# Reordered copies, GpSimd work and last tiles in a fused attention and mixer kernel (Trainium2, one core)

## The chip, the cores and the metric

The kernel runs on one core of one Trainium2 chip. The metric is the device time of one execution in microseconds (us), as the median of the executions that agree. TensorE is called PE (its weight loads PEld), VectorE DVE, ScalarE ACT, GpSimd POOL; SP issues the DMAs. A ratio is the mean time of one kernel's fast runs over that of before's fast runs of the same rounds, so it is not quite the ratio of the medians that are quoted.

## The reference, cut to what matters

```python
# q, k, v: (4, 8, 768, 64) float32; lam: (8,)
# 1. lightning attention, blocks of 64 rows, state kv carried along the sequence
out[blk] = ((q @ k.T) * Dmask) @ v + (q * lam_pow) @ kv_state
kv_state = lam_block * kv_state + (k * rev_pow).T @ v
x = out.transpose(0, 2, 1, 3).reshape(4, 768, 512)
# 2. low-rank mixing along the sequence (rank 32), then a two-layer channel product
u = x + ((x.T @ U) @ V).T                       # U, V, w_ch1, w_ch2 come as float64
y = u + maximum(u @ w_ch1, 0) @ w_ch2           # (4, 768, 512) float32
```

## The kernel before

There are 24 steps of attention, one per tile of 128 rows (4 batches of 6). A step prepares the next tile (`prep`: q and k transposed by PE, copied out of PSUM by ACT), makes the outputs of its own tile, the scores of the next, and turns its result back (`back`). A batch that is complete is mixed (`mix`: x becomes u) and turned (`turn`: u transposed for the first product and split into a high part H, a low part, and a correction D), one tile per step. The last x tiles are mixed and turned between matmuls of the first product (`rest`: unit, matmul, piece; a unit has 24 matmuls).

The names in the traces: PE transposes q and k into pq and pk, ACT copies these to qt and kt, and GpSimd scales them to qs and ks. pss are the scores, which DVE masks to sm; px is the output of attention, xt its copy on ACT, pxn the tile turned back, x_nat its copy on ACT (`back`). pkv is the new state, kvc and kv its copies. pp and pr make the low-rank sum (pt, pt_h and vp are its copies), pu is what `mix` adds to x_nat on DVE ("the add"). put holds the transposes of `turn`; ut is its high part, made on DVE, u_hl holds H and the low part, te is ut scaled, uf a plain copy of put, and u_d is D (in a DMA line it is u stored to HBM). pz and pd are the two sums of the first product, and r is made of both, first on ACT, then on DVE.

```python
def prep(s):
    ...                       # PE: transposes pq, pk;  ACT: copies qt, kt
    ks = ...; nc.gpsimd.tensor_tensor(out=ks, in0=raw[s, "k"], ...)
    qs = ...; nc.gpsimd.tensor_tensor(out=qs, in0=qt, in1=powq, op=ALU.mult)
    for name in "qk":
        load_next(name)       # loads three tiles ahead; a buffer is free when ks has read it

def turn(s):
    ...                       # PE: transposes put
    nc.vector.tensor_scalar(t, pt, HI, ...)                      # DVE: ut
    nc.scalar.copy(uhl[g][:, 0, :, cols], t)                     # ACT: H
    low, diff = uhl[g][:, 1, :, cols], ud[g][:, :, cols]
    if g >= FG:                                                  # the last eight tiles
        nc.scalar.copy(uf, pt)                                   # ACT, reads PSUM
        nc.gpsimd.tensor_tensor(out=low, in0=uf, in1=t, ...)
        nc.vector.scalar_tensor_tensor(diff, t, 1.0 + E, pt, ...)  # D, reads PSUM
    else:
        nc.vector.tensor_tensor(out=low, in0=pt, in1=t, ...)
        nc.scalar.mul(te, t, E)
        nc.gpsimd.tensor_tensor(out=diff, in0=te, in1=low, ...)  # D
    nc.sync.dma_start(out=u_d[s], in_=xs.pop(s))                 # store of u

# step s: prep(s+1), mix, [low], outputs(s), [low_sum], scores(s+1), back(s), turn
# side work (decoding float64 weights) before scores or at the end of a step
rest = [
    (0, 0, "mix", c0 - 1), (0, 1, "turn", c0 - 2), (0, 5, "low", b), (0, 10, "low_sum", b),
    (0, 18, "mix", c0), (1, 0, "turn", c0 - 1), (1, 2, "mix", c0 + 1), (1, 8, "turn", c0),
    ...                       # turnings 8 matmuls apart, each tile mixed two turnings ahead
]
```

V was loaded in two halves, each broadcast to 128 partitions and decoded by itself. x tiles live in a ring of eight buffers.

## Time and profile before

| stretch | us | what bounds it |
|---|---|---|
| start to pss of step 1 | 11.76 | loads, decay masks |
| attention (to pss of step 23) | 132.47 | PE, with some 10 us of waits |
| head of the first product (to its fourth unit) | 35.69 | DVE's chain on the last tiles |
| rest of the products | 526.88 | PE without a wait |
| span | 706.80 | device time 708.66 |

In a timeline line stand start, duration, engine, source line, operation, output<-input, shapes and count, and in brackets how long the engine sat idle before it and what it waited for. "Idle time" of PE has to be read with care, because the profile models a matmul's end; I go by starts.

### The profile page before, as it was taken

How to read it: one execution, taken by the hardware profiler on the slowest of the kernel's cores; microseconds unless marked ns; L12 is line 12 of the kernel's file. 1: busy time of each engine (PE TensorE's matmuls, PEld its weight loads, DVE VectorE, ACT ScalarE, POOL GpSimd, SP SyncE). 2: the span in 40 equal slices, each digit the busy share in tenths (PEclk: the TensorE clock that was granted, in tenths of full speed). 3: DMA queues.
4: the chain of work that ended last, by engine and by line, in shares of the span. 5: the costliest groups of instructions: out<-in, count | busy, mean ns of one | idle time of the engine just before them, and what ended most of it. 6: DMA issues, size and time to landing. Idle time of an engine off the chain costs nothing.

```text
span 706.8 us, 11409 instructions
## 1 busy us (share of the span) xinstructions
PE 687.7 (97%) x4176; PEld 556.3 (79%) x4176; DVE 506.5 (72%) x909; ACT 305.8 (43%) x545; POOL 111.7 (16%) x91
## 2 busy tenths in 40 slices
PE   7999999998999999999999999999999999999997
PEld 6878797866788888888888888888888888888886
DVE  5668786866699877777779625678676586775864
ACT  4667677753466544444446412232232232322320
POOL 4324464632200000000000000003030030300300
PEclk9999999999999999999999999999999999999999
DMA  9898878404477755665557899966345363353431
GB/s 190 169 196 196 197 168 187 118 32 164 150 251 252 260 204 195 211 206 194 193 194 268 282 325 329 372 223 208 104 123 177 94 204 105 119 181 102 163 93 59
DMA packets 131856, 131.77 MB, mean 186 GB/s; under 512 B 81368, under 2 KB 89560, under 8 KB 131800
## 3 DMA queue, kind: packets, MB, share of 16 engines
q1 hardware_dynamic: 130600, 130.77, 60.7%
q8 instruction: 33, 0.54, 0.3%
q10 hardware_dynamic: 1200, 0.27, 0.2%
q14 instruction: 23, 0.19, 0.1%
HBM read 80.68 MB, written 50.33 MB: 185 GB/s over the span
## 4 chain that ended last, share of the span: by engine, by line
PE 85%; DVE 6%; DMA 3%; ACT 3%; issue 2%; POOL 0%; ACTq 0%; SPq 0%; DVEq 0%; POOLq 0%
PE pz L582 25%; PE pz L709 13%; PE pz L707 13%; PE pd L711 13%; PE pd L589 12%; PE pss L322 2%; PE px L345 2%; DMA kraw<-in_k_dram 1%; DVE sm L328 1%; PE px L340 1%; PE pp L397 1%; DVE kvc L370 1%; PE pxn L385 1%; PE put L437 1%; DMA words<-in_moe_w_ch_dram 1%
## 5 line engine op out<-in xcount | busy, mean ns | idle before, releaser
L582 PE MATMUL pz<-u_hl,w 128*128 128x512 f32 x768 | 190.3, 398 | 1.3 <-ACT r L596 1.3
L582 PEld LDWEIGHTS pz<-u_hl,w 128*128 128x128 f32 x768 | 144.2, 188 | 37.4 <-ACT r L596 1.6
L709 PE MATMUL pz<-w_hl,m 128*128 128x512 f32 x384 | 151.6, 396 | 0.0
L707 PE MATMUL pz<-w_hl,m 128*128 128x512 f32 x384 | 151.6, 396 | 0.0
L711 PE MATMUL pd<-w_d,m 128*128 128x512 f32 x384 | 150.0, 396 | 0.0
L691 ACT ACTIVATE m<-mt 128x512 fp32r<-128x512 f32 x96 | 60.7, 632 | 196.8 <-PE pd L711 138.6
L692 DVE SCALAR_TENSOR_TENSOR m<-rm,m 128x512 fp32r<-128x512 f32 x96 | 71.5, 746 | 50.5 <-ACT m L691 50.1
L731 POOL TENSOR_TENSOR o<-o,u 128x512 f32<-128x512 f32 x20 | 29.8, 1526 | 449.0 <-DVE o L729 449.0
L597 DVE SCALAR_TENSOR_TENSOR r<-pd,r 128x512 f32<-128x512 f32 x96 | 61.8, 685 | 51.6 <-ACT r L596 45.7
L589 PE MATMUL pd<-u_d,w 128*128 128x512 f32 x384 | 98.5, 397 | 0.0
L709 PEld LDWEIGHTS pz<-w_hl,m 128*128 128x128 f32 x384 | 72.3, 188 | 17.6
L711 PEld LDWEIGHTS pd<-w_d,m 128*128 128x128 f32 x384 | 72.3, 188 | 17.6
L707 PEld LDWEIGHTS pz<-w_hl,m 128*128 128x128 f32 x384 | 72.3, 188 | 17.6
L589 PEld LDWEIGHTS pd<-u_d,w 128*128 128x128 f32 x384 | 72.1, 188 | 17.3
L596 ACT ACTIVATE r<-pz 128x512 f32<-128x512 f32 x96 | 51.8, 593 | 60.2 <-PE pz L582 60.1
L693 DVE SCALAR_TENSOR_TENSOR m<-m 128x512 fp32r<-128x512 f32 x96 | 69.1, 720 | 0.9
L690 DVE TENSOR_SCALAR mt<-rm 128x512 uint32<-128x512 uint32 x96 | 46.1, 481 | 30.2 <-DMA rm<-r_d 30.0
L345 PE MATMUL px<-sm,vraw 128*64 128x128 f32 x384 | 37.8, 275 | 0.8 <-DVE sm L328 0.7
L167 ACT CAST w<-wt 128x512 fp32r<-128x512 f32 x32 | 19.9, 622 | 34.1 <-DVE wt L164 25.8
L328 DVE TENSOR_TENSOR sm<-pss,mask 128x512 f32<-128x512 f32 x48 | 30.7, 680 | 5.0 <-PE pss L322 4.9
L340 PE MATMUL px<-qs,kv 128*64 128x128 f32 x320 | 33.6, 279 | 0.4 <-issue 0.4
L322 PE MATMUL pss<-qt,kt 64*128 64x128 f32 x384 | 28.8, 291 | 4.5 <-ACT kt L297 4.5
(81 smaller groups left out, 771.2 us busy)
## 6 DMA issues: line engine op xcount, KB each, us to landing
r_d<-r SPq DMA_DIRECT2D x96, 256.0 KB, 2.5
rm<-r_d SPq DMA_DIRECT2D x96, 256.0 KB, 2.7
words<-in_moe_w_ch_dram SPq DMA_DIRECT2D x32, 512.0 KB, 4.3
w_d<-w SPq DMA_DIRECT2D x16, 768.0 KB, 3.3
w_hl<-w_d SPq DMA_DIRECT2D x16, 512.0 KB, 6.4
u_d<-x_nat SPq DMA_DIRECT2D x24, 256.0 KB, 3.8
u<-u_d SPq DMA_DIRECT2D x24, 256.0 KB, 4.1
out_dram<-o SPq DMA_DIRECT2D x24, 256.0 KB, 2.0
```

The source lines that it names most:

```text
L345: nc.tensor.matmul(out=px[x * D : (x + 1) * D, a, :], lhsT=vr[:, 2 * a + x, :], rhs=sm[:, x, a, :], start=(c == 0), stop=True,)
L582: nc.tensor.matmul(out=acc[g][0], lhsT=w[:, n, ct, :], rhs=uhl[g][:, n, ct, :], start=(ct == 0 and n == 0), stop=(ct == CT - 1 and n == 1),)
L589: nc.tensor.matmul(out=acc[g][1], lhsT=w[:, 2, ct, :], rhs=ud[g][:, ct, :], start=(ct == 0), stop=(ct == CT - 1),)
L596: nc.scalar.mul(r, pz, 1.0 + E)
L597: nc.vector.scalar_tensor_tensor(r, pd, 4096.0, r, ALU.mult, ALU.add)
L690: nc.vector.tensor_scalar(t.bitcast(U32), r.bitcast(U32), HI, None, ALU.bitwise_and)
L691: nc.scalar.activation(out=m[:, 0], in_=t, func=AF.Relu)
L692: nc.vector.scalar_tensor_tensor(m[:, 1], r, 0.0, hi, ALU.max, ALU.subtract)
L693: nc.vector.scalar_tensor_tensor(m[:, 2], hi, E, low, ALU.mult, ALU.subtract)
L707: nc.tensor.matmul(out=pz, lhsT=m[:, 0, cols], rhs=hl[:, 0], start=first, stop=False)
L709: nc.tensor.matmul(out=pz, lhsT=m[:, 1, cols], rhs=hl[:, 1], start=False, stop=end)
L711: nc.tensor.matmul(out=pd, lhsT=m[:, 2, cols], rhs=dd, start=first, stop=end)
```

## The change

The intent is to keep PE fed in attention and in the head of the first product. ACT copies q and k before u's H; GpSimd makes D, then qs, then the next tile's ks; V is loaded and decoded once, on 64 partitions; D of the last tiles follows ut directly, and the last x tile is turned back inside the first product. Side work moves to the start of a step, and half of the decoding of a third part of w_ch1 (`w1_2`), done in the first product before, comes into attention (steps 15 and 21 to 23).

```diff
@@ prep @@
-        if c < NT - 1:  ks = ...; nc.gpsimd.tensor_tensor(out=ks, ...)
-        if c > 0:       qs = ...; nc.gpsimd.tensor_tensor(out=qs, ...)
+    def scale_k(s): ...            # ks of tile s
+    def scale(s):                  # qs of tile s, then
+        if s + 1 < NS:
+            scale_k(s + 1)
@@ turn @@
-        nc.scalar.copy(uhl[g][:, 0, :, cols], t)
         if g >= FG:
+            nc.vector.scalar_tensor_tensor(diff, t, 1.0 + E, pt, ALU.mult, ALU.subtract)
+            nc.scalar.copy(hi, t)
             nc.scalar.copy(uf, pt)
             nc.gpsimd.tensor_tensor(out=low, in0=uf, in1=t, op=ALU.subtract)
-            nc.vector.scalar_tensor_tensor(diff, t, 1.0 + E, pt, ALU.mult, ALU.subtract)
...
+        def rest():                # runs in the next step, behind prep
+            nc.scalar.copy(hi, t)
+            nc.scalar.mul(te, t, E)
+            nc.gpsimd.tensor_tensor(out=diff, in0=te, in1=low.bitcast(FP32), op=ALU.subtract)
+            nc.sync.dma_start(out=u_d[s], in_=xs.pop(s))
+        turned[s] = rest
@@ a step @@
         step = [("prep", s + 1)] * (s + 1 < NS)
+        step += [("turned", done - 1)] * (done > 0)
+        step += [("scale", s + 1)] * (s + 1 < NS)
+        step += [("aside", s)]     # side work, now here
...
-        (v_steps(0), (0, -3, 3, 3, 3, 4, 4)),
-        (v_steps(1), (2, -5, 5, 6, 6, -7, 7)),
-        (w1_steps(0), (7, -8, -9, -10, -11, -13, -14, -15)),
+        (v_steps(), (0, 3, 3, 4, 4, 5, 5, 6)),
+        (w1_steps(0), (3, 7, 8, 9, 10, 11, 12, 13)),
...
@@ rest @@
+        (0, 0, "mix", c0 - 1), (0, 4, "back", NS - 1), (0, 4, "enter", None),
+        (0, 4, "turn", c0 - 2), (0, 9, "low", b), (0, 14, "low_sum", b),
+        (0, 18, "turn", c0 - 1), (0, 22, "mix", c0),
+    at = [(1, 6), (1, 13), (1, 20), (2, 6), (2, 13), (2, 20)]
+    for n, (unit, i) in enumerate(at):
+        rest.append((unit, i, "turn", c0 + n))
+        if n + 1 < NT:
+            rest.append((unit, i + 1, "mix", c0 + n + 1))
```

More of the change, by code (lines that the diff above doesn't have):

```diff
@@ L90, in tmp, with weight_steps, load_pieces @@
         return wconv.tile([P, C], FP32, tag="tmp", bufs=3, name=name)
-    def weight_steps(dst, src, n):
+    def weight_steps(dst, src, n, rows=P):
         st = {}
-        dims = "p (c f) -> p c f" if len(src.shape) == 3 else None
-        def shape(t, f):
-            return t.rearrange(dims, f=f) if dims else t
+        src = src if isinstance(src, list) else [src]
+        plain = src[0].dtype == FP32
+        def load_pieces(t):
+            at = 0
+            for piece in src:
+                piece = piece if plain else piece.bitcast(U32)
+                part = t[at : at + piece.shape[0]]
+                if len(piece.shape) == 3:
+                    part = part.rearrange("p (c f) -> p c f", f=piece.shape[-1])
+                nc.sync.dma_start(out=part, in_=piece)
+                at += piece.shape[0]
         def fetch():
-            if src.dtype == FP32:
-                nc.sync.dma_start(out=shape(dst(), src.shape[-1]), in_=src)
+            if plain:
+                load_pieces(dst())
                 return
             words_pool.append(words_pool.pop(0))
-            words = words_pool[-1].tile([P, 2 * C], U32, tag="words", name="words")[:, 0 : 2 * n]
-            s = src.bitcast(U32)
-            nc.sync.dma_start(out=shape(words, s.shape[-1]), in_=s)
+            words = words_pool[-1].tile([P, 2 * C], U32, tag="words", name="words")
+            words = words[0:rows, 0 : 2 * n]
+            load_pieces(words)
             st["w"] = words.rearrange("p (n two) -> p n two", two=2)
         def one():
-            if src.dtype == FP32:
+            if plain:
                 return
             hi = st["w"][:, :, 1]
-            st["sc"] = sc = wconv.tile([P, C], U32, tag="sc", name="sc")[:, 0:n]
-            st["m"] = m = wconv.tile([P, C], U32, tag="m", name="m")[:, 0:n]
+            st["sc"] = sc = wconv.tile([P, C], U32, tag="sc", name="sc")[0:rows, 0:n]
+            st["m"] = m = wconv.tile([P, C], U32, tag="m", name="m")[0:rows, 0:n]
             sc_f = sc.bitcast(FP32)
@@ L122, in one @@
             nc.vector.tensor_scalar(m, hi, 0xFFFFF, 0x100000, ALU.bitwise_and, ALU.bitwise_or)
-            nc.scalar.activation(out=sc_f, in_=sc, func=AF.Relu, bias=ends[-1][:, 0:1], scale=-1.0)
+            low_end, high_end = ends[-1][0:rows, 0:1], ends[-1][0:rows, 1:2]
+            nc.scalar.activation(out=sc_f, in_=sc, func=AF.Relu, bias=low_end, scale=-1.0)
             nc.scalar.activation(
-                out=sc, in_=sc_f, func=AF.Relu, bias=ends[-1][:, 1:2], scale=-float(1 << 23)
+                out=sc, in_=sc_f, func=AF.Relu, bias=high_end, scale=-float(1 << 23)
             )
         def two():
-            if src.dtype == FP32:
+            if plain:
                 return
@@ L137, in three @@
         def three():
-            if src.dtype == FP32:
+            if plain:
                 return
@@ L143, in four @@
         def four():
-            if src.dtype == FP32:
+            if plain:
                 return
@@ L279, in make_gather @@
             nc.vector.tensor_copy(out=gather[:, g, :], in_=gather[:, 0, :])
+    r_pool = None
     xs = {}
@@ L285, in prep @@
     def prep(s):
-        b, c = divmod(s, NT)
         qt, kt = (att.tile([P, HP, P], FP32, tag=n, bufs=2, name=n) for n in ("qt", "kt"))
@@ L297, in prep, with scale_k @@
                 nc.scalar.copy(dst[:, a0 : a0 + n, :], pt)
-        qs = ks = None
-        if c < NT - 1:
-            ks = att.tile([P, HP, 2, D], FP32, tag="ks", bufs=2, name="ks")
+        st[s].update(qt=qt, kt=kt)
+        for name in "qk":
+            load_next(name)
+    def scale_k(s):
+        st[s] = {}
+        if s % NT < NT - 1:
+            st[s]["ks"] = ks = att.tile([P, HP, 2, D], FP32, tag="ks", bufs=2, name="ks")
             nc.gpsimd.tensor_tensor(
@@ L306, in prep @@
             )
-        if c > 0:
-            qs = att.tile([P, HP, P], FP32, tag="qs", bufs=2, name="qs")
-            nc.gpsimd.tensor_tensor(out=qs, in0=qt, in1=powq, op=ALU.mult)
-        st[s] = [qt, kt, qs, ks]
-        del raw[s, "q"], raw[s, "k"]
-        for name in "qk":
-            load_next(name)
+    def scale(s):
+        if s % NT > 0:
+            st[s]["qs"] = qs = att.tile([P, HP, P], FP32, tag="qs", bufs=2, name="qs")
+            nc.gpsimd.tensor_tensor(out=qs, in0=st[s]["qt"], in1=powq, op=ALU.mult)
+        if s + 1 < NS:
+            scale_k(s + 1)
     def scores(s):
-        qt, kt = st[s][0:2]
+        qt, kt = st[s]["qt"], st[s]["kt"]
         pss = [bank([P, HP, P], "pss") for x in range(2)]
@@ L328, in scores @@
             nc.vector.tensor_tensor(out=sm[:, x], in0=pss[x], in1=mask[:, x], op=ALU.mult)
-        st[s].append(sm)
+        st[s]["sm"] = sm
     def outputs(s):
         b, c = divmod(s, NT)
-        qs, sm, vr = st[s][2], st[s][4], raw[s, "v"]
+        qs, sm, vr = st[s].get("qs"), st[s]["sm"], raw[s, "v"]
         px = bank([P, HP, P], "px")
@@ L356, in state @@
         if c < NT - 1:
-            ks, vr = st[s][3], raw[s, "v"]
+            ks, vr = st[s]["ks"], raw[s, "v"]
             pkv = bank([P, HP, D], "pkv")
@@ L423, in mix @@
         nc.vector.tensor_tensor(out=xs[s], in0=pu, in1=xs[s], op=ALU.add)
-    uhl, ud = {}, {}
+    uhl, ud, turned = {}, {}, {}
     hl_at, d_at = [hl_pool], [d_pool]
@@ L441, in turn @@
         nc.vector.tensor_scalar(t.bitcast(U32), pt.bitcast(U32), HI, None, ALU.bitwise_and)
-        nc.scalar.copy(uhl[g][:, 0, :, cols], t)
-        low, diff = uhl[g][:, 1, :, cols], ud[g][:, :, cols]
+        hi, low, diff = uhl[g][:, 0, :, cols], uhl[g][:, 1, :, cols], ud[g][:, :, cols]
         if g >= FG:
+            nc.vector.scalar_tensor_tensor(diff, t, 1.0 + E, pt, ALU.mult, ALU.subtract)
             uf = tmp("uf").rearrange("p (c n) -> p c n", n=P)
+            nc.scalar.copy(hi, t)
             nc.scalar.copy(uf, pt)
             nc.gpsimd.tensor_tensor(out=low, in0=uf, in1=t, op=ALU.subtract)
-            nc.vector.scalar_tensor_tensor(diff, t, 1.0 + E, pt, ALU.mult, ALU.subtract)
-        else:
-            nc.vector.tensor_tensor(out=low, in0=pt, in1=t, op=ALU.subtract)
+            nc.sync.dma_start(out=u_d[s], in_=xs.pop(s))
+            return
+        nc.vector.tensor_tensor(out=low, in0=pt, in1=t, op=ALU.subtract)
+        def rest():
             te = tmp("te").rearrange("p (c n) -> p c n", n=P)
+            nc.scalar.copy(hi, t)
             nc.scalar.mul(te, t, E)
             nc.gpsimd.tensor_tensor(out=diff, in0=te, in1=low.bitcast(FP32), op=ALU.subtract)
-        nc.sync.dma_start(out=u_d[s], in_=xs.pop(s))
-    pieces = [("prep", 0), ("scores", 0)]
+            nc.sync.dma_start(out=u_d[s], in_=xs.pop(s))
+        turned[s] = rest
+    pieces = [("prep", 0), ("scale", 0), ("scores", 0)]
     for s in range(NS):
         b, c = divmod(s, NT)
+        done = s - NT - 1
         step = [("prep", s + 1)] * (s + 1 < NS)
-        step += [("mix", s - NT - 1)] * (s > NT)
+        step += [("turned", done - 1)] * (done > 0)
+        step += [("scale", s + 1)] * (s + 1 < NS)
+        step += [("aside", s)]
+        step += [("mix", done)] * (done >= 0)
         step += [("low", b - 1)] * (c == 0 and b > 0)
@@ L468 @@
         step += [("low_sum", b - 1)] * (c == 0 and b > 0)
-        step += [("scores", s + 1)] * (s + 1 < NS)
-        step += [("back", s)]
-        done = s - NT - 1
-        if done >= 0 and done // TG < FG:
-            step += [("turn", done)]
+        step += [("scores", s + 1), ("back", s)] * (s + 1 < NS)
+        step += [("turn", done)] * (done >= 0 and done // TG < FG)
         pieces += step
@@ L484, with v_steps @@
         "low": low, "low_sum": low_sum, "mix": mix, "turn": turn,
+        "scale": scale, "turned": lambda s: turned.pop(s)(),
     }
-    def v_steps(half):
-        cols = slice(half * SH, (half + 1) * SH)
+    def v_steps():
         st = {}
@@ L491, in dst, with parts @@
             if "v" not in st:
-                st["v"] = wconv.tile([P, C], FP32, tag="wf", name="vf")[:, 0:SH]
+                st["v"] = wconv.tile([P, C], FP32, tag="wf", name="vf")[0 : 2 * R, 0:SH]
             return st["v"]
+        def parts(gs):
+            for half in range(2):
+                rows, cols = slice(half * R, (half + 1) * R), slice(half * SH, (half + 1) * SH)
+                for g in gs:
+                    yield v_hl[g * R : (g + 1) * R, cols], rows
         def five():
-            st["t"] = t = wconv.tile([P, C], FP32, tag="wt", name="vt")[:, 0:SH]
+            st["t"] = t = wconv.tile([P, C], FP32, tag="wt", name="vt")[0 : 2 * R, 0:SH]
             nc.vector.tensor_scalar(
@@ L499, in five, with low @@
             )
-            for g in range(0, G, 2):
-                rows = slice(g * R, (g + 1) * R)
-                nc.scalar.copy(v_hl[rows, cols], t[rows])
-        def six():
-            for g in range(1, G, 2):
-                rows = slice(g * R, (g + 1) * R)
+            for out, rows in parts((0, 2)):
+                nc.scalar.copy(out, t[rows])
+        def low(g):
+            for out, rows in parts((g,)):
                 nc.vector.tensor_tensor(
-                    out=v_hl[rows, cols], in0=st["v"][rows], in1=st["t"][rows], op=ALU.subtract
+                    out=out, in0=st["v"][rows], in1=st["t"][rows], op=ALU.subtract
                 )
-        return weight_steps(dst, moe_V[:, cols].unsqueeze(0).broadcast_to([G, R, SH]), SH) + [five, six]
+        halves = [moe_V[:, half * SH : (half + 1) * SH] for half in range(2)]
+        return weight_steps(dst, halves, SH, 2 * R) + [five, lambda: low(1), lambda: low(3)]
     u_side = weight_steps(
@@ L517, with aside @@
     side = {}
-    first, early, late = [], {}, {}
+    w1_2 = w1_steps(2)
     for steps, at in (
-        (u_side, (None, 1, 1, 1, 1)),
-        (v_steps(0), (0, -3, 3, 3, 3, 4, 4)),
-        (v_steps(1), (2, -5, 5, 6, 6, -7, 7)),
-        (w1_steps(0), (7, -8, -9, -10, -11, -13, -14, -15)),
-        (w1_steps(1), (11, -16, -17, -19, -20, -21, -22, -23)),
+        (u_side, (-1, 2, 2, 2, 2)),
+        (v_steps(), (0, 3, 3, 4, 4, 5, 5, 6)),
+        (w1_steps(0), (3, 7, 8, 9, 10, 11, 12, 13)),
+        (w1_steps(1), (5, 14, 15, 16, 17, 18, 19, 20)),
+        (w1_2[:4], (15, 21, 22, 23)),
     ):
         for step, n in zip(steps, at):
-            if n is None:
-                first.append(step)
-            else:
-                (early if n < 0 else late).setdefault(abs(n), []).append(step)
+            side.setdefault(n, []).append(step)
+    side[4].append(make_gather)
+    def aside(s):
+        for step in side.pop(s, ()):
+            step()
     ordered = ctx.enter_context(ExitStack())
@@ L538, with enter_first_product @@
         load_next(name)
-    for step in first:
-        step()
+    aside(-1)
     constants()
-    for i, (what, s) in enumerate(pieces):
+    scale_k(0)
+    run["aside"] = aside
+    for what, s in pieces:
         run[what](s)
-        if i == 1:
+        if (what, s) == ("scores", 0):
             powers()
-        if what == "outputs":
-            for step in early.pop(s, ()):
-                step()
-        if i + 1 == len(pieces) or pieces[i + 1][0] == "prep":
-            n = pieces[i - 1][1] if what == "turn" else s
-            for step in late.pop(n, ()):
-                step()
-            if n == 3:
-                make_gather()
-    assert not early and not late
-    att_ctx.close()
-    words_pool[:] = [wconv]
-    for pools, name in ((hl_at, "hl_b"), (d_at, "d_b")):
-        pools.append(ctx.enter_context(tc.tile_pool(name=name, bufs=NG - FG, reuse_waits="tile")))
-    r_pool = ctx.enter_context(tc.tile_pool(name="r", bufs=5, reuse_waits="tile"))
-    set_ends(r_pool.tile([P, 2], FP32, tag="ends", bufs=1, name="ends"))
+    assert not side
+    def enter_first_product(s):
+        nonlocal r_pool
+        att_ctx.close()
+        words_pool[:] = [wconv]
+        for pools, name in ((hl_at, "hl_b"), (d_at, "d_b")):
+            pools.append(
+                ctx.enter_context(tc.tile_pool(name=name, bufs=NG - FG, reuse_waits="tile"))
+            )
+        r_pool = ctx.enter_context(tc.tile_pool(name="r", bufs=5, reuse_waits="tile"))
+        set_ends(r_pool.tile([P, 2], FP32, tag="ends", bufs=1, name="ends"))
     def banks():
@@ L636 @@
     rest = [
-        (0, 0, "mix", c0 - 1), (0, 1, "turn", c0 - 2), (0, 5, "low", b), (0, 10, "low_sum", b),
-        (0, 18, "mix", c0), (1, 0, "turn", c0 - 1), (1, 2, "mix", c0 + 1), (1, 8, "turn", c0),
-        (1, 12, "mix", c0 + 2), (1, 16, "turn", c0 + 1), (1, 20, "mix", c0 + 3),
-        (2, 0, "turn", c0 + 2), (2, 4, "mix", c0 + 4), (2, 8, "turn", c0 + 3),
-        (2, 12, "mix", c0 + 5), (2, 16, "turn", c0 + 4), (2, 22, "turn", c0 + 5),
-    ]
+        (0, 0, "mix", c0 - 1), (0, 4, "back", NS - 1), (0, 4, "enter", None),
+        (0, 4, "turn", c0 - 2), (0, 9, "low", b), (0, 14, "low_sum", b),
+        (0, 18, "turn", c0 - 1), (0, 22, "mix", c0),
+    ]
+    at = [(1, 6), (1, 13), (1, 20), (2, 6), (2, 13), (2, 20)]
[3 more added lines that the diff above has]
+            rest.append((unit, i + 1, "mix", c0 + n + 1))
+    run["enter"] = enter_first_product
     head = [(pair, ft) for two in (pairs[:2], pairs[2:]) for ft in (0, 1) for pair in two]
-    side = list(zip((0, 1, 2, 2, 3, 3, 4, 4), w1_steps(2)))
+    side = list(zip((2, 3, 3, 4), w1_2[4:]))
     for i, (pair, ft) in enumerate(head):
```

## The prediction

> **What bounds the kernel now.** I read the page first. Section 1 gives PE 97% busy; section 4, the chain that ended last, gives PE 85% of the span:
>
> ```profile
> PE 687.7 (97%) x4176; PEld 556.3 (79%) x4176; DVE 506.5 (72%) x909; ACT 305.8 (43%) x545; POOL 111.7 (16%) x91
> PE 85%; DVE 6%; DMA 3%; ACT 3%; issue 2%; POOL 0%; ACTq 0%; SPq 0%; DVEq 0%; POOLq 0%
> ```
>
> The chain in order of time then shows pure matmul pieces (3.75 us of pz, 1.88 us of pd) from 180 us to the end. The diff touches none of that code, so some 527 us stay as they are. Before 180 us the chain hops between DVE, ACT, DMA and PE. That stretch has two parts: attention with its side work (to 144 us) and the head of the first product, with the last six x tiles mixed and turned inside it (144 to 180 us). Only waits there can be won. The waits of the weight loads, up to 182 us (engine, line, waited for, us, times, longest):
>
> ```profile
> PEld pss L322 <- ACT kt L297: 6.2, 10, 1.2
> PEld put L437 <- DVE x_nat L423: 3.6, 3, 2.0
> PEld px L345 <- DVE sm L328: 2.1, 6, 0.4
> PEld pz L582 <- ACT r L596: 1.6, 1, 1.6
> PEld pxn L385 <- ACT xt L350: 1.0, 1, 1.0
> ```
>
> I then listed the starts of pss (one per step) in the PE timeline and took the shortest step of each kind as its pure PE length: 4.91 us without mixing, 5.6 with mixing, 4.24 or 4.93 for the last step of a batch (no pkv), 6.93 or 7.6 for a step with the low-rank sum. From 11.76 to 144.23 us this makes about 122.6 us against 132.5 taken: **9.9 us lost**. Step 3 to 4 loses 2.0 (q and k from DMA), 5 to 6 loses 1.9, 9 to 10 1.6, 11 to 12 and 17 to 18 1.2 each, six others 0.3 each; the rest is rounding.
>
> Why kt is late is seen in the ACT timeline, steps 10 and 11:
>
> ```profile
> 68.43 0.62 ACT L442 CAST u_hl<-ut 128x512 fp32r<-128x512 f32 x1 [1.35 <-DVE ut L441]
> 68.96 0.63 ACT L453 ACTIVATE te<-ut 128x512 f32<-128x512 f32 x1
> 69.49 0.57 ACT L297 COPY qt<-pq 128x512 f32<-128x512 f32 x1
> 69.95 0.59 ACT L297 COPY kt<-pk 128x512 f32<-128x512 f32 x1
> ...
> 74.54 0.62 ACT L442 CAST u_hl<-ut 128x512 fp32r<-128x512 f32 x1 [1.57 <-DVE ut L441]
> ```
>
> ACT is idle 1.35 us, although pq and pk were transposed at 66.6 to 67.5 us, because its next instruction is u's H, which waits for ut on DVE, which stands behind sm. Only then come qt and kt, and pss starts at 70.59. It is a loop: pss, side step on DVE, sm, ut, H, te, qt, kt, next pss. It takes 5.9 to 6.1 us where PE needs 5.6.
>
> In the tail the loss is on DVE:
>
> ```profile
> 163.09 0.69 DVE L449 SCALAR_TENSOR_TENSOR u_d<-ut,put 128x512 fp32r<-128x512 f32 x1 [1.17 <-ACT uf L446]
> 163.69 0.68 DVE L423 TENSOR_TENSOR x_nat<-pu,x_nat 128x512 f32<-128x512 f32 x1
> 164.29 0.68 DVE L441 TENSOR_SCALAR ut<-put 128x512 uint32<-128x512 uint32 x1
> 166.15 0.69 DVE L449 SCALAR_TENSOR_TENSOR u_d<-ut,put 128x512 fp32r<-128x512 f32 x1 [1.17 <-ACT uf L446]
> ```
>
> Every turned tile costs DVE 3.06 us (163.09 to 166.15), of which 1.17 is a wait for ACT's copy uf. DVE waits so for 8.8 us in 7 times. It falls behind, and put on PE waits for the mixed x 3.6 us.
>
> **What the Trainium skill says.** "PSUM — Partial Sum Buffer", section "PSUM bank collisions raise a hardware error": no two engines may touch one bank at once, ScalarE and VectorE both reading included, so such accesses must be ordered. The trace agrees: D (L449) reads put, needs nothing from uf, and still starts only after uf, which reads the same bank. "TensorE: Matmul & The Clock Gate", section "Architectural detail": the queues of ScalarE and VectorE are strict first-in first-out, and TensorE pulls only weight loads forward. The trace agrees: qt and kt stand behind a waiting H for 1.35 us. "Perfetto Trace Analysis", section "Tensor Engine Instruction": the end of a matmul is computed. Hence I count starts on PE; its "97% busy" hides part of the stalls. "DMA: Bandwidth & Descriptors", "Specifications": transfers under 512 B miss line rate. Rows of q, k, v are 256 B, and the first 46 us move 180 GB/s at 95% or more of DMA time, against 372 in the best slice.
>
> **The change part by part.**
>
> *qt and kt ahead of H and te (attention).* No instruction is added. With pq at time 0 of a step, pk ends near 0.9, qt and kt are done by 1.8, and pss starts at 3.66 at the soonest (0.88 for pq and pk, 0.43 pu, 1.69 px, 0.66 pkv). kt gets almost 2 us of slack. The kt waits sum to 6.2 us, all of which should go. H and te now end near 2.9, before xt is wanted (3.2). ACT's work per step is 0.62+0.62+0.57+0.59+0.60+0.83+0.59 = 4.4 us, so it fits in 5.6.
>
> *GpSimd order D, qs, next ks.* 1.28+1.28+1.06 = 3.6 us per step, as before. D waits for te (2.9), qs ends near 5.5, wanted at 6.9 by the next px: it fits. The k loads no longer wait for ks of the same step (35.0 us of the DMA queue's waits, 10 times); mostly hidden behind three buffers, but it helps step 4.
>
> *V once.* Before: two fetches of 384 KB, two conversions. After: one fetch of 192 KB on 64 partitions. DVE saves one conversion, 0.35+0.35+0.55+0.56+0.56 and 0.34 for the mask, 2.7 us; ACT 0.61+0.62. The four copies and four subtractions stay. The fetch also moves behind q and k of step 4: they gain 384 KB / 180 GB/s = 2.2 us, which covers the 2.0 us lost at step 4.
>
> *Side steps.* They leave the place between kvc and sm and run at the start of a step; w1's words come at 3 and 5 instead of 7 and 11, so DVE no longer waits for words at 59.3 us (that held back sm at step 9 to 10). The DVE sum with a side step of 0.7 to 1.5 is 4.2+1.5 = 5.7 at worst, 5.0 typically. Against it: gather (2.3 us of DVE) now delays kvc in step 4, and V's four copies (2.1 us of ACT) stand before xt in step 5: I estimate 0.3 and 0.6 us of stall.
>
> Sum for attention: of 9.9 us lost I expect 2 to 3 to remain: **about 7 us won** (1.8 at step 4, 1.3 at step 5, 1.6 at step 9, 2.3 of the rest).
>
> *Last tiles: D behind H.* D is emitted before uf, so DVE does ut, D, add back to back, 0.6+0.6+0.6 = 1.9 us a tile instead of 3.06. PE work from pss at 144.23 on is 4.0 us to the end of px; 10.1 us for unit 0 (24 matmuls of 0.2345, low 1.84, sum 0.9, two transposes 0.88, two mixings 0.46, back 0.39), 7.6 and 7.4 for units 1 and 2: 29.2 us against 35.7 now, **6.5 lost**. back of the last step now stands behind four matmuls, which covers its 1.0 us wait. What remains: mixing n+1 comes one matmul after turning n, and turning n+1 seven later. From put: 0.66 to ut, then ut, D, add to 2.55; PE comes back at 2.31. So 0.25 to 0.5 us remain in each of five turnings, 1.5 us. **About 5 us won.**
>
> Total 12 us; I take 11.5 for small new waits: 708.66 - 11.5 = 697.2 us.
>
> **Rivals.** (1) *DMA becomes the bound of early attention.* From 11.76 to 46.5 us it is busy 95%; the change saves 576 KB but draws w1's two fetches (1 MB) into it. Against: k and q are three steps ahead, and PE needs 768 KB per 4.91 us, 164 GB/s. If it bites, 2 to 3 us return: 700. (2) *The x ring.* u_d is now stored in the step after, behind q and k in the queue, and back of the same step reuses, of eight x tiles, the one that store reads. Issue near 2 us plus 3.8 (up to 5.4) to land gives 5.8 to 7.4, while ACT wants to write at 5.4. kt of the next step tolerates some 2 us. If it bites often: 702. (3) *DVE or GpSimd takes the bound.* Some DVE side operations take 1.46 or 1.55 instead of 0.68 us beside GpSimd work, and 5.7 us is at PE's step: up to 2 us, 699. (4) *All waits go*: 708.7 - 16.4 = 692.3, the floor, since no PE work is removed.
>
> **Range and chances.** Over 2% faster needs below 694.5, that is 14.2 of the 16.4 us of waits; I named 3 to 5 us that should stay, so 0.14. Slower needs a new wait of 26 us: 0.01. Range 693.8 to 702.0, from nearly all won to rivals 1 and 2 together.
>
> **What will show it.** pss no longer waits for kt, and steps with mixing take 5.6 to 5.7 us; pq of step 4 does not wait for q; L449's successor never waits for uf, and put's waits are below 2 us; the fourth unit starts near 168.5 instead of 180. Wrong if ACT's x_nat waits for u_d, if px waits for qs or kv, or if q's DMA waits move to steps 7 to 10.

## The result, and the profile after

The changed kernel takes **699.87 us** (median of 4 runs, 699.27 to 700.57) against 708.71; the ratio is 0.9874, 95% interval 0.9857 to 0.9891. The result is correct. The prediction was 697.2 us in a range of 693.8 to 702.0, so the time lies in the range; of the 11.5 us forecast, 8.8 came.

| stretch | before | after | won | forecast |
|---|---|---|---|---|
| start to pss of step 1 | 11.76 | 11.87 | -0.1 | 0 |
| attention | 132.47 | 125.77 | 6.7 | about 7 |
| head of the first product | 35.69 | 33.26 | 2.4 | about 5 |
| rest | 526.88 | 526.90 | 0.0 | 0 |

Nearly all of what is missing is in the head. These are the engines' row and the chain's row of the page after the change:

```profile
PE 684.1 (98%) x4176; PEld 555.3 (80%) x4176; DVE 501.5 (72%) x903; ACT 305.6 (44%) x543; POOL 108.0 (15%) x91
PE 88%; DVE 4%; ACT 3%; DMA 2%; issue 1%; POOL 0%; ACTq 0%; DVEq 0%; POOLq 0%
```

PE's share of the chain rises from 85 to 88%. The waits of the weight loads, up to 175 us (waited for: us in total, times, longest):

```profile
PEld put L456 <- ACT uf L467: 4.6, 4, 1.6
PEld pxn L404 <- ACT xt L369: 2.6, 4, 1.4
PEld px L364 <- DVE sm L347: 0.8, 2, 0.4
PEld pss L341 <- ACT kt L310: 0.2, 1, 0.2
```

The wait for kt has gone from 6.2 to 0.2 us, the wait of px for sm from 2.1 to 0.8. But put, the transposes of the last tiles, waits longer than before (4.6 against 3.6 us), and pxn waits for xt 2.6 us. ACT's timeline in attention after the change shows the new order at work:

```profile
93.38 0.59 ACT L406 COPY x_nat<-pxn 128x512 f32<-128x512 f32 x1 [1.25 <-DMA u_d<-x_nat]
93.86 0.59 ACT L310 COPY qt<-pq 128x512 f32<-128x512 f32 x1
94.34 0.60 ACT L310 COPY kt<-pk 128x512 f32<-128x512 f32 x1
94.97 0.62 ACT L476 CAST u_hl<-ut 128x512 fp32r<-128x512 f32 x1
95.49 0.62 ACT L477 ACTIVATE te<-ut 128x512 f32<-128x512 f32 x1
```

qt and kt stand ahead of H and te, so no DVE result is between pq and kt. Two successive starts of pss in mixed steps are now 5.59 us apart (84.59 to 90.18 us, for instance), where it had been up to 5.9 to 6.1. The first line shows something new: the copy x_nat waits for the store of u that still reads its buffer.

The head of the first product, all engines (put at 156.98 turns x tile 19, put at 159.88 tile 20):

```profile
156.98 0.63 PE L456 MATMUL put<-ident,x_nat 128*128 128x128 f32 x4 [0.86 <-ACT uf L467]
157.72 0.69 DVE L460 TENSOR_SCALAR ut<-put 128x512 uint32<-128x512 uint32 x1 [0.88 <-PE put L456]
158.45 0.69 DVE L464 SCALAR_TENSOR_TENSOR u_d<-ut,put 128x512 fp32r<-128x512 f32 x1
159.05 0.68 DVE L442 TENSOR_TENSOR x_nat<-pu,x_nat 128x512 f32<-128x512 f32 x1
159.24 0.59 ACT L467 COPY uf<-put 128x512 f32<-128x512 f32 x1 [0.18 <-DVE u_d L464]
159.88 0.63 PE L456 MATMUL put<-ident,x_nat 128*128 128x128 f32 x4 [0.41 <-ACT uf L467]
```

D (L464) no longer waits for uf: DVE does ut, D and the add of the next tile in one go. Yet DVE is now idle 0.88 us before ut, waiting for PE, and PE is idle before put. Each waits for the other once per tile: put to put takes 2.90 us. The profile names ACT's uf as what put waited for. The add of tile 20 ends at 159.73 and uf at 159.83 us, only 0.1 us apart, so this label had to be tested.

### The profile page after: what moved, and what is told of

Same layout as the page of the kernel before. It is cut to its first block, busy times and chain, and to the rows that moved or that the text cites. A ratio compares the mean times of both kernels' runs of the same rounds, so it can differ in the third digit from the quotient of the medians.

```text
span 697.8 us, 11361 instructions
## 1 busy us (share of the span) xinstructions
PE 684.1 (98%) x4176; PEld 555.3 (80%) x4176; DVE 501.5 (72%) x903; ACT 305.6 (44%) x543; POOL 108.0 (15%) x91
## 4 chain that ended last, share of the span: by engine, by line
PE 88%; DVE 4%; ACT 3%; DMA 2%; issue 1%; POOL 0%; ACTq 0%; DVEq 0%; POOLq 0%
PE pz L613 25%; PE pz L745 13%; PE pz L743 13%; PE pd L747 13%; PE pd L620 12%; PE pss L341 2%; PE px L364 2%; PE px L359 2%; DMA u_d<-x_nat 2%; PE pxn L404 1%; PE put L456 1%; PE pkv L380 1%; DVE ut L460 1%; PE pk L306 1%; PE pq L306 1%
## 5 line engine op out<-in xcount | busy, mean ns | idle before, releaser
L364 PE MATMUL px<-sm,vraw 128*64 128x128 f32 x384 | 36.1, 274 | 0.3 <-DVE sm L347 0.2
L359 PE MATMUL px<-qs,kv 128*64 128x128 f32 x320 | 32.2, 279 | 0.0
L136 ACT ACTIVATE sc<-sc,ends 128x512 f32<-128x512 uint32 x29 | 21.0, 724 | 19.2 <-DVE sc L132 19.2
```

The source lines that it names most:

```text
L364: nc.tensor.matmul(out=px[x * D : (x + 1) * D, a, :], lhsT=vr[:, 2 * a + x, :], rhs=sm[:, x, a, :], start=(c == 0), stop=True,)
```

## The experiments

Two theories were open for put's waits. **A1**: uf, which runs after D because both read one PSUM bank, releases the bank that the next put needs. **A2**: the next put waits for its own x, whose add stands behind ut and D in DVE's queue, because mixing n+1 comes after turning n. A rival to both was that the turnings are merely too close. For attention the theory was that each part takes away the wait it was meant for; the rivals were that the waits move.

### 1. The six last turnings spread over three units

```diff
-    at = [(1, 6), (1, 13), (1, 20), (2, 6), (2, 13), (2, 20)]
+    at = [(1, 4), (1, 14), (2, 0), (2, 10), (2, 20), (3, 8)]
```

> After, with the six last turnings spread over units 1 to 3 of the first product, 10 to 12 matmuls apart instead of 7. Theory A (each turning needs about 2.9 us from put through ut, D and uf to the next put, while PE has 2.31 us of work between two puts, so PE waits): with 10 matmuls PE has about 3.0 us of work, the waits of put (4.6 us) fall below 1.0 us, and the kernel gains 3 to 3.6 us against after, 696.3 to 696.9 us. Rival (the wait only moves: unit 4 then waits for the low part of the last tile, or the r pieces at the start of a unit hold the turning up): under 1 us gained, over 698.9 us.

Measured: 698.81 us (698.72 to 698.89), ratio 0.9854: 1.1 us won, near the rival's figure and far from the 3 to 3.6 expected. The waits of the weight loads between 136 and 180 us, and the pieces at the start of unit 1 on DVE and PE:

```profile
PEld put L456 <- ACT uf L467: 2.2, 3, 1.0
PEld pz L613 <- POOL u_hl L468: 0.9, 1, 0.9
...
154.28 1.29 DVE L628 SCALAR_TENSOR_TENSOR r<-pd,r 128x512 f32<-128x512 f32 x2 [0.63 <-ACT r L627]
155.49 0.68 DVE L460 TENSOR_SCALAR ut<-put 128x512 uint32<-128x512 uint32 x1
```

Where a turning falls near the start of a unit, ut (put ran at 153.84) stands behind r's two pieces of the unit that just ended, 1.29 us, and these wait 0.63 us for ACT. Put to put is then 3.79 us (153.84 to 157.63), more than 10 matmuls and a mixing can fill. A clean turning needed 3.03 us and did not wait. And the last tile, moved into unit 3, comes too late for unit 4, which waits 0.9 us for its low part. Spacing alone is not the cure.

### 2. Mixing n+1 just ahead of turning n

```diff
-        rest.append((unit, i, "turn", c0 + n))
         if n + 1 < NT:
-            rest.append((unit, i + 1, "mix", c0 + n + 1))
+            rest.append((unit, i, "mix", c0 + n + 1))
+        rest.append((unit, i, "turn", c0 + n))
```

> After, with the mixing of tile n+1 put just ahead of the turning of tile n instead of one matmul behind it, so that the add of n+1 stands before ut and D of n on VectorE. Theory A1 (the next put waits for uf, which releases the PSUM bank): the waits of put stay at 4 to 5 us and the time within 0.5 us of after. Theory A2 (the next put waits for its add, which stands behind D, as the prediction had it): the waits fall to 1 to 2 us, 2.5 to 3.5 us gained, about 697 us.

Measured: 696.64 us (696.31 to 696.85), ratio 0.9823: 3.2 us won over the changed kernel, as A2 has it; the head takes 29.92 in place of 33.26 us. Put's waits fall from 4.6 to 0.8 us. The timeline (put at 156.70 turns tile 19, put at 159.00 tile 20):

```profile
156.70 0.60 PE L456 MATMUL put<-ident,x_nat 128*128 128x128 f32 x4
157.27 0.68 DVE L442 TENSOR_TENSOR x_nat<-pu,x_nat 128x512 f32<-128x512 f32 x1
157.88 0.68 DVE L460 TENSOR_SCALAR ut<-put 128x512 uint32<-128x512 uint32 x1
158.59 0.69 DVE L464 SCALAR_TENSOR_TENSOR u_d<-ut,put 128x512 fp32r<-128x512 f32 x1
159.00 0.60 PE L456 MATMUL put<-ident,x_nat 128*128 128x128 f32 x4
159.46 0.59 ACT L467 COPY uf<-put 128x512 f32<-128x512 f32 x1 [0.25 <-POOL u_hl L468]
```

The add of tile 20 (157.27) is ahead of ut and D of tile 19. Put of tile 20 starts at 159.00, 0.46 us before uf of tile 19 even begins, with 2.30 us from put to put: it does not need uf. In the compiled program of the changed kernel too, the transposes of tiles 18, 19 and 20 lie in PSUM banks 0, 7 and 0, so put of 20 does not reuse the bank that uf of 19 reads. Its two wait counts there are the add of tile 20 on DVE and, on ACT, uf of tile 18, which had ended at 156.94 us; none of the four puts that wait needs uf of the tile just before it. A1 falls; the label "ACT uf" was a coincidence of 0.1 us.

### 3. The old places of mixing and turning, D still behind H

```diff
-        (0, 18, "turn", c0 - 1), (0, 22, "mix", c0),
-    at = [...]  (and its loop)
+        (0, 18, "mix", c0), (1, 0, "turn", c0 - 1), (1, 2, "mix", c0 + 1), (1, 8, "turn", c0),
+        (1, 12, "mix", c0 + 2), (1, 16, "turn", c0 + 1), (1, 20, "mix", c0 + 3),
+        ...                       # as before the change
```

> After, with the places of the last mixings and turnings as they were before (each tile mixed two turnings ahead, turnings 8 matmuls apart), D still behind H. Theory A1: PE has 2.55 us between two puts against 2.9 us, so 0.35 us of wait in each of five, plus the r pieces, 2.5 to 3.5 us of put waits in place of 4.6, 698.5 to 699.5 us. Theory A2: no wait is left but at the last turning, 696.5 to 697.5 us. If the new places were what won in the tail: slower than after by 1 us or more.

Measured: 697.54 us (696.84 to 697.93), ratio 0.9835: 2.3 us faster than the changed kernel. No put waits at all; only one pu waits 1.2 us for the low-rank sum, which now has less time. The new places of the change cost 2.3 us against the old ones (2.7 by the head alone, 33.26 against 30.52). This agrees with A2 and is the plainest sign that D's move, not the new places, won in the head.

### 4 and 12. Before, with only D moved behind H

```diff
         if g >= FG:
+            nc.vector.scalar_tensor_tensor(diff, t, 1.0 + E, pt, ALU.mult, ALU.subtract)
             uf = tmp("uf").rearrange("p (c n) -> p c n", n=P)
             nc.scalar.copy(uf, pt)
             nc.gpsimd.tensor_tensor(out=low, in0=uf, in1=t, op=ALU.subtract)
-
-            nc.vector.scalar_tensor_tensor(diff, t, 1.0 + E, pt, ALU.mult, ALU.subtract)
```

> Before, with one line moved: D of the last eight tiles right behind H, ahead of the copy uf. Theory: VectorE's wait for uf (8.8 us, 7 times) goes, its cycle of 3.06 us a tile falls to 2.55 (PE bound) or 2.9 (put to put), put's waits fall from 3.6 to 1.5 to 3 us and the wait of pz for r (1.6 us) goes: 2.5 to 4 us gained on before, 704.7 to 706.2 us. Rival (VectorE was not the limit, PE waits for the same bank anyway): under 1 us gained.

Measured: 703.89 us, ratio 0.9926, 4.6 us won on before: more than expected. Its profiled execution was an outlier, 1363.37 us, in which 16 matmuls of pz took 7.60 us where before's take 3.91; the other five executions ran 703.34 to 704.31. The kernel was run again.

> The fourth experiment once more, because its profiled run was an outlier with a halved TensorE rate and its trace shows no tail that can be read: the time again 703.3 to 704.4 us; VectorE's waits for uf gone from the list, and put's waits between 144 and 180 us below 1.5 us (the time already says that 4.6 us were won), the fourth unit starting near 175.3 us.

Measured: 703.99 us (703.50 to 704.64), ratio 0.9933. DVE's timeline in the head:

```profile
161.38 0.69 DVE L445 SCALAR_TENSOR_TENSOR u_d<-ut,put 128x512 fp32r<-128x512 f32 x1
161.99 0.68 DVE L423 TENSOR_TENSOR x_nat<-pu,x_nat 128x512 f32<-128x512 f32 x1
162.60 0.69 DVE L441 TENSOR_SCALAR ut<-put 128x512 uint32<-128x512 uint32 x1
163.32 0.69 DVE L445 SCALAR_TENSOR_TENSOR u_d<-ut,put 128x512 fp32r<-128x512 f32 x1
```

A tile costs DVE 1.94 us (161.38 to 163.32) in place of 3.06. DVE never waits for uf, no put waits, and unit 4 starts at 174.78 instead of 179.92 us. One moved line gives half of the whole change's gain.

### 5. Before, with only q and k copied ahead of H

```diff
-        nc.scalar.copy(uhl[g][:, 0, :, cols], t)
...                               # H, te and D of the first 16 tiles become rest()
+        step += [("turned", s - NT - 2)] * (s - NT - 1 > 0)     # behind prep
```

> Before, with the copies of q and k ahead of u's H and te alone (H, te and D are emitted behind the transposes of the next step; GpSimd then has ks, qs, D; the store of u stays where it was; V as before). Theory: the waits of pss for kt fall from 6.2 us to about 1.5 (step 5 to 6 stays, there V's copies stand ahead of them), the mixed steps take 5.6 to 5.7 us in place of 5.9 to 6.1, 4 to 5 us gained on before, 703.7 to 704.7 us; the step with the late words (9 to 10) keeps its wait for sm, and step 3 to 4 its DMA wait. Rival (the loop moves to another wait, xt or kv): under 2 us gained.

Measured: 705.13 us (704.04 to 706.85), ratio 0.9953: 3.4 us won, a little under the 4 to 5 expected. Its waits of the weight loads:

```profile
PEld put L437 <- DVE x_nat L423: 3.6, 3, 2.0
PEld pss L322 <- ACT kt L297: 1.2, 2, 0.9
```

The kt wait falls from 6.2 to 1.2 us; the head's put wait is untouched, as it should be. The mixed steps take 5.59 us. What stays is step 3 to 4 (7.03 us, DMA), 5 to 6 (6.12) and 9 to 10 (6.73, sm behind late words), which other parts of the change take care of.

### 6. Before, with only V loaded once

The loader and decoder of V are those of the change; V is fetched where its first half was and split in step 4.

> Before, with V loaded and converted once on 64 partitions, fetched where the first half was (ahead of q and k of step 4), split in step 4. Theory: 576 KB less to load, one conversion less (2.7 us of VectorE, 1.2 us of ScalarE), but these stand beside other work; q and k of step 4 come 1 us sooner (192 KB at 180 GB/s): 1 to 1.5 us gained, 707.2 to 707.7 us. If the load of V is the whole of the wait at step 4: 2 us or more gained.

Measured: 707.06 us (706.62 to 708.57), ratio 0.9987, interval 0.9974 to 1.0001: 0.9 us by the ratio, 1.5 by the medians, not clear of nothing. The profile says why: step 3 to 4 is now without a wait (4.91 us between the pss at 21.20 and 26.11), 2.0 us won as if V's load were the whole of that wait, with the fetch still in its old place; but step 5 to 6 takes 7.16 us instead of 6.12, because V's four copies on ACT now stand together ahead of kt (1.97 us of wait). One wait was traded for half of another.

### 7. After, with the store of u back in the turning

```diff
         nc.vector.tensor_tensor(out=low, in0=pt, in1=t, op=ALU.subtract)
+        nc.sync.dma_start(out=u_d[s], in_=xs.pop(s))
         def rest():
...
-            nc.sync.dma_start(out=u_d[s], in_=xs.pop(s))
```

> After, with u stored to HBM right behind the low part in the turning (as before the change) and not with H in the next step. Theory (the ring of eight x tiles: the copy x_nat waits for the store that reads its tile, 8.1 us of ScalarE in 5 times, which makes xt and pt late in the steps of 11 to 18): ScalarE's wait for the store falls below 1 us, the step 18 to 19 takes 7.6 in place of 8.5 us, 0.8 to 1.3 us gained on after, 698.6 to 699.1 us. Rival (hidden by the slack of kt): under 0.4 us.

Measured: 698.52 us (698.24 to 698.63), ratio 0.9858: 1.3 us won on the changed kernel. The line of ACT's waits that it takes away, from the changed kernel:

```profile
ACT x_nat L406 <- DMA u_d<-x_nat: 8.1, 5, 2.2
```

It is not in this kernel's list at all. The step 18 to 19 takes 7.61 instead of 8.46 us, 12 to 13 7.61 instead of 7.75. Attention is 1.0 us shorter (124.77 against 125.77), so most of the 8.1 us never reached PE and about an eighth did.

### 8. After, with V's copies split over two steps

```diff
-        (v_steps(), (0, 3, 3, 4, 4, 5, 5, 6)),
+        (v_steps(), (0, 3, 3, 4, 4, 5, 6, 5, 6)),   # copies of group 0 in step 5, of 2 in step 6
```

> After, with V's four copies on ScalarE split over two steps (two in step 5, two in step 6). Theory: they stand before xt in step 5 and make pxn wait 1.4 us at 38.4 us; split, xt comes 1.03 us sooner, and in step 6 there is room before pt: 0.8 to 1.2 us gained on after, 698.7 to 699.1 us. Rival (pt of step 6 becomes late and pr waits): 0 to 0.4 us.

Measured: 698.99 us (698.87 to 699.12), ratio 0.9865: 0.9 us won, in the theory's range, but with part of the rival. The waits of the weight loads, 11 to 182 us:

```profile
PEld pr L425 <- ACT pt L421: 1.2, 2, 0.6
PEld pxn L404 <- ACT xt L369: 1.1, 4, 0.3
```

pxn's wait falls from 2.6 to 1.1 us, pr's rises from 0.6 to 1.2. Step 6 to 7 takes 7.01 instead of 8.19 us; step 12 to 13 takes 8.59 instead of 7.75, in the profiled run, because x_nat waits longer for a store there (up to 3.1 us). So of the 1.2 us won between steps 5 and 7, attention as a whole keeps 0.2 in that run (125.56 us), and 0.5 us more lies before step 1, where the edit changes nothing: that the total fell into the theory's range is in part luck. Experiment 9 shows the split again without the store's wait.

### 9. Three edits together

Edits 2 and 7, and V's split one step earlier: its mask and two copies in step 4, the other two copies and gather in step 5.

```diff
-        (v_steps(), (0, 3, 3, 4, 4, 5, 5, 6)),
-    side[4].append(make_gather)
+        (v_steps(), (0, 3, 3, 4, 4, 4, 5, 5, 6)),
+    side[5].append(make_gather)
```

> After, with three edits together: each mixing ahead of the turning (as in the second experiment), the store of u behind the low part (as in the seventh), and V's split moved one place: its mask and two copies in step 4, the other two copies and gather in step 5. If the three waits are independent: 3.2 + 1.1 + 1.2 to 1.5 us off after, 694.0 to 694.6 us, over 2% faster than before (below 694.5). If they share a limit (ScalarE's order, DMA): 695.5 us or more.

Measured: 694.14 us (693.91 to 694.42), ratio 0.9791, interval 0.9775 to 0.9807: 5.7 us faster than the changed kernel and 14.4 faster than before, correct. The three waits are independent, as expected: the head takes 29.93 us, as in experiment 2, and attention 123.92, of which the store gives 1.0 us (124.77 in experiment 7) and V's split the other 0.8; the interval just reaches past 0.98, so "over 2%" itself stays unclear by a hair.

### 10. After, with GpSimd's order as before

```diff
     def scale(s):
+        scale_k(s)                # ks of the same tile, ahead of qs
         if s % NT > 0:
             ...                   # qs
-        if s + 1 < NS:
-            scale_k(s + 1)
```

> After, with GpSimd's order as before the change in each step: D, then ks and qs of the same step (ks not a step early). Theory (GpSimd has time: 3.6 of 5.6 us): qs ends near 6.6 us after the step's start, wanted at 6.9, so px waits for qs 0 to 0.3 us in some steps, and the loads of k wait for ks again, hidden by three buffers: 0 to 1 us slower than after, 699.9 to 700.9 us. If the GpSimd order is a main part of the gain: 2 us or more slower.

Measured: 729.70 us (729.46 to 730.62), ratio 1.0294: **30 us slower** than the changed kernel and 21 slower than before. Neither theory named this. The timeline of ACT, GpSimd and SP through one step, and SP's wait for ks from the list of waits:

```profile
63.28 1.27 POOL L475 TENSOR_TENSOR u_d<-te,u_hl 128x512 fp32r<-128x512 f32 x1 [5.48 <-PE pss L338]
64.52 1.05 POOL L318 TENSOR_TENSOR ks<-kraw,small 128x512 f32<-128x512 f32 x1
...
65.60 0.37 SPq L231 DMA_DIRECT2D kraw<-in_k_dram  x1
66.07 0.52 SPq L476 DMA_DIRECT2D u_d<-x_nat  x1
...
69.48 0.58 ACT L403 COPY x_nat<-pxn 128x512 f32<-128x512 f32 x1 [5.07 <-DMA u_d<-x_nat]
...
72.30 1.28 POOL L475 TENSOR_TENSOR u_d<-te,u_hl 128x512 fp32r<-128x512 f32 x1 [5.49 <-ACT te L474]
...
SPq L231 <- POOL ks L318: 57.6, 11, 6.7
```

It is a closed loop of 9.02 us (63.28 to 72.30) where PE needs 5.6. D waits for te; ks stands behind D; the load of k waits for ks, because it overwrites what ks reads; the store of u stands behind that load in SP's queue; x_nat waits for the store, since it reuses the x tile; and behind x_nat on ACT stand qt, kt, H and te. SP waited for ks 57.6 us in 11 times, ACT for the store 39.1 us in 11 times. With ks a step early the load of k is not held, and the loop is open. So GpSimd's new order is not a nicety: once the store of u is behind q's and k's loads, it is what makes that place bearable. Experiment 5 had ks ahead of D and the store in the turning, and no such loop. That the old order with the store in the turning would do for the full change is likely from this, but was not run.

### 11. After, with the last x turned back at the end of attention

```diff
-        step += [("scores", s + 1), ("back", s)] * (s + 1 < NS)
+        step += [("scores", s + 1)] * (s + 1 < NS) + [("back", s)]
-        (0, 0, "mix", c0 - 1), (0, 4, "back", NS - 1), (0, 4, "enter", None),
+        (0, 0, "mix", c0 - 1), (0, 4, "enter", None),
```

> After, with the last x turned back at the end of attention as before, not behind four matmuls of the first product. Theory: pxn waits for xt again, 0.9 to 1.0 us, all on PE's path: 0.7 to 1.0 us slower than after, 700.6 to 700.9 us. Rival (the wait is made up for by the waits of put behind it): under 0.3 us.

Measured: 701.33 us (700.91 to 702.06), ratio 0.9893: 1.5 us slower by the medians, 1.3 by the ratios, somewhat more than expected. pxn's waits for xt rise from 2.6 to 3.6 us, which is the 1.0 us of the theory, and the head takes 34.02 in place of 33.26 us, 0.8 longer. The rest is not the edit's: in the profiled run attention took 1.0 us longer (126.80 against 125.77), most of it in step 12 to 13 (8.52 in place of 7.75), whose code is the same in both and where ACT waits for a store; the start was 0.3 us shorter.

## Why the prediction was right, and where it was not

**What bounds it** held: the 527 us behind the head did not move by more than 0.02 us, and everything happened in the first 180 us. The range was wide, 8.2 us beside a forecast gain of 11.5, and took in what went missing in the head.

**qt and kt ahead of H** held: the wait for kt went from 6.2 to 0.2 us, mixed steps take 5.59 us, and alone the part gives 3.4 us (experiment 5).

**V once** held at step 4, which lost its 2.0 us wait (also alone, experiment 6). Experiment 6 left the fetch where it was, so the smaller load was enough and the new place was not needed for it. The price was mis-sized: I put 0.6 us on V's four copies ahead of xt in step 5, and they cost 1.5 us (steps 5 to 6 and 6 to 7 take 0.27 and 1.26 more than their pure PE length). Experiment 8 moves half of them and wins 0.9.

**Side steps** held: the step 9 to 10, which had lost 1.6 us to late words, takes 5.59 us. gather did no visible harm. In sum attention keeps 3.2 us of waits (125.77 - 122.6), where I expected 2 to 3.

**GpSimd's order** was judged wrongly. I wrote that the k loads' wait for ks was "mostly hidden behind three buffers". It was in before; with the store of u behind these loads it is not, and the order is worth 30 us as a guard (experiment 10). I had the two pieces, this one and rival 2, and did not join them into a loop.

**Rival 2, the x ring**, came true mildly: x_nat waited 8.1 us, of which 1.0 to 1.3 us reached the end (experiment 7). It was also a sign that the prediction had named for being wrong, "if ACT's x_nat waits for u_d". Rivals 1 and 3 did not show. No transpose of q or k waits for its load after 9.1 us, and from 11.9 to 46 us the DMAs moved 219 GB/s, so the 180 GB/s seen before were no ceiling; px waits 0.4 us for qs and 0.8 for sm.

**D behind H** held in its mechanism: alone it gives 4.6 us, and DVE's cycle then falls to 1.94 us as computed (1.9). The prediction did not size it alone.

**The step that failed** is the term "So 0.25 to 0.5 us remain in each of five turnings, 1.5 us." The chain put, ut, D, add, put was the right one (experiment 2 shows that it is the add and not uf), but its size was wrong: 3.6 us stayed, not 1.5 (itself near the low end of five times 0.25 to 0.5). Four of the five stretches from put to put had 2.31 us of PE work and took 3.32, 2.90, 3.70 and 2.90 us; the fifth (tile 20 to 21, 3.03 us) has ten matmuls in it, which the prediction overlooked, and did not wait. There are two reasons. The chain takes 2.90 us, not 2.55: ut starts 0.74 us after put, D 0.73 after ut, and put comes 0.15 us after the add's end. And where a unit ends, r's two pieces, 1.29 us and 0.63 us of waiting for ACT, stand before ut, which gives the 3.32 and the 3.70 us (153.66 to 156.98, 162.91 to 166.61). In the head 4.1 us are left over (33.26 - 29.2); the half microsecond beyond the 3.6 I have not placed. This is nearly the whole of what the forecast of 11.5 us had too much. Before the change each tile had been mixed two turnings ahead, so the chain did not exist; the new places made it. The prediction did not compare them with the old ones, which with D moved leave no wait of put: they cost 2.3 us (experiment 3). Two of its own signs say the same: put's waits were to fall below 2 us and were 4.6, and the fourth unit was to start near 168.5 us and started at 170.9.

**back behind four matmuls** held: 0.8 us in the head (experiment 11; 1.3 to 1.5 by the times, with attention's variation in them), I had put 1.0.

The parts alone do not add up exactly: 4.6 (D) + 3.4 (q, k) + 0.9 to 1.5 (V) + 0.8 to 1.5 (back) - 2.3 (places) is 7.4 to 8.7 us, against 8.8 measured; the places of the side steps were not run alone.

## What to carry to other kernels

When a wait is taken out of an in-order queue, write down the new chain from one use to the next through every engine, with what stands in each queue at that place, and compare its length with the work that the bounding engine has in between; emit the producer of the next item ahead of the consumer of this one. A late DMA issue can hold an unrelated one behind it in the same queue, so a buffer ring, a load's wait and a store's place must be looked at together. And a wait with several semaphores carries the name of whatever ended last: when two candidates are 0.1 us apart, look up in the compiled program what is waited for, or move one and see.

## What the Trainium skill lacked or had wrong

- "PSUM — Partial Sum Buffer", "PSUM bank collisions raise a hardware error": the rule agrees with the trace, but the page does not say what two readers of one bank cost in order: here DVE sat idle 1.17 us a tile, 8.8 us in 7 times, and moving one instruction won 4.6 us.
- "Perfetto Trace Analysis", "Identifying Dependency Chains": it tells the reader to look at the semaphores waited for, but not that, with several, the last event on an engine can be a coincidence. Here uf, 0.1 us behind the add, was named for 4.6 us of waits and was not their cause (experiment 2: 3.2 us won without touching uf); the counts in the compiled program named the right uf, two tiles earlier.
- "DMA: Bandwidth & Descriptors": I found nothing there on an issue that waits for a semaphore holding back later, unrelated issues of the same queue. Here it held the store of u behind the load of k and cost 30 us (SP waited 57.6 us, ACT 39.1 us).
- "TensorE: Matmul & The Clock Gate" explains a halved rate by idleness, and warns that clock events in a trace can be unreliable. One execution of 1363.37 us had matmuls at half the rate (7.60 against 3.91 us for 16) through dense work, with a granted clock of 1.000 in the record; whether that record is wrong no run here shows, and I found no page that gives a cause.
